# Gate stores issued by GpSimd, low-rank pieces fetched a tile ahead, features loaded in pieces, 49-point operands padded

## The chip, the cores and the metric

One core of a Trainium2 chip. The metric is device microseconds of one launch; less is better.

## What is computed

Three blocks, each feeding the next, on tensors of batch 2, 3136 tokens, 256 features (float32):

```python
# 1 attention with squared ReLU scores, gated by u
attn = np.maximum(np.matmul(z, z.transpose(0, 2, 1)) / S, 0.0) ** 2
x = u * np.matmul(attn, v)
# 2 low-rank token mixing (rank 32), then a channel MLP of width 1024
u1 = x + (x.transpose(0, 2, 1) @ U @ V).transpose(0, 2, 1)
y = u1 + np.maximum(u1 @ w_ch1, 0.0) @ w_ch2
# 3 2-D Fourier mixing (tokens and features), layer norm, a second channel MLP
u2 = y + np.real(np.fft.fft(np.fft.fft(y, axis=1), axis=2))
un = (u2 - mean(u2)) / np.sqrt(var(u2) + 1e-6)
out = u2 + np.maximum(un @ w2_ch1, 0.0) @ w2_ch2
```

U, V and the MLP weights arrive as float64 and are converted on the chip. Every large product is made of three matmuls: operands are split into an upper part `h` and a remainder `l` (ScalarE copies to the upper part, VectorE subtracts), and h·h, h·l and l·h are summed in PSUM. The 3136-point token transform is a 64 x 49 split; `b49h` and `b49l` are the two parts of the 49-point matrix, 98 rows (49 points, two parities) by 128 columns.

## The kernel before

Tokens are cut into seven chunks of 448 (`CH`) per batch. The program has two parts, each with an order of work written out by hand as Python generators that are advanced step by step. Within a part every engine keeps the written order; where the two parts meet, a queue can take the second part's instruction first if the first part's is not yet free to run.

*Attention.* For each of 14 (batch, chunk) pairs there are 13 steps (`order`), one per pair of key tiles; the seventh step is the odd tile 12, half as wide. In a step `ahead` issues the score matmuls for two steps later (`LAG`), ScalarE takes ReLU (L542) and square (L545), VectorE casts to `h` (L546) and subtracts for `l` (L96, the line of the helper `sub`), and `values` does the 24 matmuls onto the accumulators (L568). On the eleventh key tile of each pair, `gate` multiplies with u and writes the result to DRAM twice: feature-major to `aT_d` by one DMA (L599) and, after a 32 x 32 transpose by VectorE (L602), token-major to `aN_d` by eight DMAs (L606). Each of those eight moves 32 partitions x 14 blocks x 32 floats. All of them are issued by SP (`load` is `nc.sync.dma_start`, `late_dma` is `nc.gpsimd.dma_start`), and SP also issues all the loads of the following steps: queries, keys, values and u, and `stg`, the weight blocks that the `conversions` jobs turn from float64 into float32. A DMA instruction on SP holds up what is written behind it.

During the second batch's attention, `lowrank` makes the 64 x 256 sum U^T x of the first batch: 13 pieces of up to 256 tokens, each loaded from `aN_d` (L620), split, and multiplied (L632) into a score bank. A piece takes four of the generator's turns: load and two yields, split and one yield, matmuls and one yield. Generators get no turn in the last two steps of a pair.

*Channel mixers.* 28 chunks (two layers, two batches, seven chunks) of eight steps. A step i does `hidden(k)`, six matmuls of the first MLP matrix (L324 to L326), and `project(k)` of step i - 2, six of the second (L349 to L351). `Chunk.prep` of the next chunk runs beside it: for layer 1 it starts at step 2 of the chunk before, adds the low-rank term by two matmuls with the V rows (L244; the rows come by `Chunk.load`, two DMAs of GpSimd, L230) to the features `xT`. The features are loaded by `load_x` (L801) in four DMAs, of 1344, 1344, 1568 and 1568 tokens, all issued before the first step. Beside the first steps `mixer` makes the low-rank sum of the second batch: 13 pieces loaded from `aN_d` into the two buffers of `wst` (L812), split into `nh` and `nl`, and multiplied (L825) one tile per step, the first in its fourth turn. `fourier(b)` later transposes 98-column pieces by TensorE (L868), splits them into 98 partitions of `nh`, `nl` and multiplies by `b49h`, `b49l` (L875 to L877). `starts` says at which step a generator begins; TensorE's program is in order, so a matmul of a generator that waits holds up those of the MLP behind it.

Of the kernel before, what the change touches and what calls it, by code (L numbers as in the profile page):

```python
# [21 lines left out]
CH = 448  # L22
# [60 lines left out]
def program(ctx, tc, zT, v, uT, U, V, w1a, w2a, w1b, w2b, b49, f64, fd, rep, mask, out):  # L83
# [8 lines left out]
    def hcopy(o, i):  # L92
        nc.scalar.copy(o, i)  # L93
# [33 lines left out]
    b49h = const.tile([98, 128], F32R, name="b49h")  # L127
    b49l = const.tile([98, 128], F32R, name="b49l")
# [8 lines left out]
    def constants(t):  # L137
        make_identity(nc, ident)
        load(out=repc, in_=rep)
        load(out=maskc, in_=mask)  # L140
        load(out=t[0:98, 0:128], in_=b49)
        load(out=f64s, in_=f64)
        load(out=t[:, 256:768], in_=fd)
        nc.vector.memset(t[:, 768:896], 1.0 / D)
        for _ in range(5):
            yield
        hcopy(ones, t[:, 768:896])
        hcopy(b49h, t[0:98, 0:128])
        sub(b49l, t[0:98, 0:128], f(b49h))
        for dst, k in ((fA, 256), (fB, 384)):  # L150
            hcopy(dst[:, 0], t[:, k : k + 128])
            sub(dst[:, 1], t[:, k : k + 128], f(dst[:, 0]))
        hcopy(fN, t[:, 512:768].rearrange("p (a n) -> p a n", a=2))
# [226 lines left out]
    def attention(stack):  # L380
# [209 lines left out]
        def gate(b, qc):  # L590
            last = (b, qc) == (1, NC - 1)
            t, tb = (ptile() if last else att.tile([128, 2 * CH], F32, tag="aT", name="aT") for _ in range(2))
            o, u = acc.pop((b, qc)), uq.pop((b, qc))
            for a in range(2):
                hcopy(c2(t)[:, a], o[a][0][:, 0:CH])
                tt(out=c2(t)[:, a], in0=o[a][1][:, 0:CH], in1=c2(t)[:, a], op=ALU.add)
            tt(out=c2(t), in0=c2(t), in1=u, op=ALU.mult)
            tokens = slice(qc * CH, qc * CH + CH)
            load(out=aT_d[b][:, :, tokens].rearrange("a p n -> p a n"), in_=c2(t))  # L599
            yield  # L600

            nc.vector.transpose(out=tb, in_=t)  # L602
            for a in range(2):
                for i in range(4):
                    o = a * 128 + i * 32
                    load(  # L606
                        out=aN_d[b][tokens, o : o + 32].rearrange("(j t) d -> t j d", t=32),
                        in_=c2(tb)[i * 32 : i * 32 + 32, a].rearrange("p (j d) -> p j d", d=32),
                    )
            yield  # L610

        def lowrank():
# [3 lines left out]
            for k in range(0, 25, 2):  # L616
# [4 lines left out]
                yield  # L621
                yield
# [5 lines left out]
                yield  # L628
# [12 lines left out]
                yield  # L641
# [129 lines left out]
    def pair_late():  # L771
        return [late["mp"].tile([128, 512], F32R, tag=t, name=t) for t in ("nh", "nl")]

# [24 lines left out]
    late["small"] = small  # L798

# [3 lines left out]
    def mixer():  # L803
# [3 lines left out]
        for k in range(28):  # L807
# [18 lines left out]
            yield  # L826
        P = small()[:, 0:D]
# [8 lines left out]
    def fourier(b):  # L836
# [27 lines left out]
        def tokens(i):  # L864
# [4 lines left out]
            h, l = (t[0:98] for t in pair_late())  # L869
            hcopy(h, ps[0:98, :])  # L870
            sub(l, ps[0:98, :], f(h))
# [14 lines left out]
        def column128():  # L886
# [3 lines left out]
            h, l = (t[0:98, 0:32] for t in pair_late())  # L890
            hcopy(h, ps[0:98, 0:32])
            sub(l, ps[0:98, 0:32], f(h))
# [158 lines left out]
    with tc.manual_schedule():  # L1051
        nstep = len(chunks) * 8
        active = []
        starts = {
            20: weights(0), 50: fourier(0), 106: fourier(1), 13 * 8: weights(1),
# [3 lines left out]
        for b, s, e in ((0, CH, 1792), (0, 1792, S), (1, 0, 1568), (1, 1568, S)):  # L1059
            load_x(b, s, e)  # L1060
        mix1 = mixer()
        active.append(mix1)
        for i in range(nstep + 2):
# [17 lines left out]
            if i in starts:  # L1081
                active.append(starts[i])
            for g in list(active):
# [49 lines left out]
```

## Time and profile before

| | us |
|---|---|
| median of 3 runs (lowest, highest) | 1226.63 (1224.61, 1229.32) |
| the profiled execution's own time | 1227.88 |
| its span, first to last instruction | 1226.1 |
| TensorE busy | 1175.5 |
| VectorE busy | 853.0 |
| ScalarE busy | 658.8 |
| GpSimd busy | 53.0 |
| mean granted TensorE clock | 0.986 |

Engines: PE is TensorE's matmuls, PEld its weight loads, DVE VectorE, ACT ScalarE, POOL GpSimd, SP SyncE. An engine name with a q is its sequencer, which waits or issues. A granted clock of 1.00 is 2.4 GHz, 0.50 is 1.2 GHz. Matmuls overlap in the record: one of 448 columns is shown with 0.36 us, while the next starts 0.20 us after it, or 0.10 us where two of 64 rows run side by side. So a busy TensorE need not be at its full pace.

### The profile page before, as it was taken

How to read it: one execution, taken by the hardware profiler on the slowest of the kernel's cores; microseconds unless marked ns; L12 is line 12 of the kernel's file. 1: busy time of each engine (PE TensorE's matmuls, PEld its weight loads, DVE VectorE, ACT ScalarE, POOL GpSimd, SP SyncE). 2: the span in 40 equal slices, each digit the busy share in tenths (PEclk: the TensorE clock that was granted, in tenths of full speed). 3: DMA queues.
4: the chain of work that ended last, by engine and by line, in shares of the span. 5: the costliest groups of instructions: out<-in, count | busy, mean ns of one | idle time of the engine just before them, and what ended most of it. 6: DMA issues, size and time to landing. Idle time of an engine off the chain costs nothing.

```text
span 1226.1 us, 21429 instructions
## 1 busy us (share of the span) xinstructions
PE 1175.5 (96%) x8454; PEld 1069.4 (87%) x8454; DVE 853.0 (70%) x1611; ACT 658.8 (54%) x1089; POOL 53.0 (4%) x104
## 2 busy tenths in 40 slices
PE   9999999899999998999499999999999999999998
PEld 8888898789889887999499899999998989899997
DVE  7877787667788887877355646466566688766674
ACT  7877777667676766766133324333255444444442
POOL 0000100000000000000000000020000111000000
PEclk9999999999999999999799999999999999999999
DMA  4313432133243233223722001111012211111111
GB/s 141 84 33 83 101 78 64 36 105 100 53 106 88 74 92 105 75 62 78 250 58 73 25 16 43 59 40 40 8 36 73 60 41 33 38 31 38 31 39 45
DMA packets 116659, 80.79 MB, mean 66 GB/s; under 512 B 63630, under 2 KB 110640, under 8 KB 116560
## 3 DMA queue, kind: packets, MB, share of 16 engines
q1 hardware_dynamic: 110448, 71.94, 20.4%
q0 software_dynamic: 5696, 7.31, 2.8%
q8 instruction: 66, 1.08, 0.4%
q14 instruction: 33, 0.27, 0.1%
q10 hardware_dynamic: 416, 0.20, 0.1%
HBM read 52.94 MB, written 26.39 MB: 65 GB/s over the span
## 4 chain that ended last, share of the span: by engine, by line
PE 68%; DVE 12%; ACT 7%; DMA 6%; SPq 4%; issue 3%; DVEq 0%; ACTq 0%
PE psO L568 20%; PE psH L324 7%; PE psH L326 6%; PE psH L325 6%; PE psC L349 6%; PE psC L350 6%; PE psC L351 6%; PE psS L536 5%; SPq L606 3%; ACT P L542 3%; ACT P L545 2%; DVE l L96 2%; DVE h L546 1%; DVE aT L602 1%; DVE Hl L330 1%
## 5 line engine op out<-in xcount | busy, mean ns | idle before, releaser
L568 PE MATMUL psO<-h,Vt 64*128 64x448 f32 x2744 | 438.0, 368 | 5.4 <-DVE h L546 5.0
L568 PEld LDWEIGHTS psO<-h,Vt 64*128 64x128 f32 x2744 | 289.8, 187 | 27.7 <-DVE h L546 8.4
L568 PE MATMUL psO<-l,Vt 64*128 64x448 f32 x1372 | 287.1, 371 | 6.5 <-DVE l L96 6.4
L330 DVE SCALAR_TENSOR_TENSOR Hl<-psH,Hh 128x448 fp32r<-128x448 f32 x224 | 138.8, 622 | 156.2 <-ACT Hh L329 155.2
L96 DVE TENSOR_TENSOR l<-P,h 128x896 fp32r<-128x896 f32 (+2 forms) x211 | 210.0, 995 | 23.7 <-ACT h L93 16.5
L329 ACT ACTIVATE Hh<-psH 128x448 fp32r<-128x448 f32 x224 | 121.2, 542 | 180.3 <-PE psH L326 177.8
L542 ACT ACTIVATE P<-psS 128x896 f32<-128x896 f32 (+1 forms) x183 | 161.0, 880 | 46.5 <-PE psS L536 44.6
L568 PEld LDWEIGHTS psO<-l,Vt 64*128 64x128 f32 x1372 | 153.8, 187 | 23.5 <-DVE l L96 15.2
L545 ACT ACTIVATE P<-P 128x896 f32<-128x896 f32 (+1 forms) x183 | 168.4, 921 | 5.7
L324 PE MATMUL psH<-h,w 128*128 128x448 f32 x448 | 168.1, 375 | 0.0
L326 PE MATMUL psH<-h,w 128*128 128x448 f32 x448 | 164.6, 367 | 0.0
L325 PE MATMUL psH<-l,w 128*128 128x448 f32 x448 | 164.5, 367 | 0.0
L349 PE MATMUL psC<-Hh,w 128*128 128x448 f32 x448 | 163.9, 366 | 0.3 <-DVE P L372 0.2
L350 PE MATMUL psC<-Hl,w 128*128 128x448 f32 x448 | 163.6, 365 | 0.4 <-DVE Hl L330 0.4
L351 PE MATMUL psC<-Hh,w 128*128 128x448 f32 x448 | 162.7, 363 | 0.0
L546 DVE CAST h<-P 128x896 fp32r<-128x896 f32 (+1 forms) x183 | 110.3, 603 | 70.3 <-ACT P L545 68.3
L536 PE MATMUL psS<-Q,KT 64*128 64x448 f32 x1002 | 135.3, 367 | 5.6 <-ACT P L542 3.1
L536 PEld LDWEIGHTS psS<-Q,KT 64*128 64x128 f32 x1002 | 100.5, 186 | 13.8 <-ACT P L542 4.2
L349 PEld LDWEIGHTS psC<-Hh,w 128*128 128x128 f32 x448 | 84.2, 188 | 8.3 <-issue 1.2
L350 PEld LDWEIGHTS psC<-Hl,w 128*128 128x128 f32 x448 | 84.3, 188 | 8.2 <-DVE Hl L330 1.4
L324 PEld LDWEIGHTS psH<-h,w 128*128 128x128 f32 x448 | 84.6, 189 | 7.4 <-issue 0.3
L326 PEld LDWEIGHTS psH<-h,w 128*128 128x128 f32 x448 | 84.4, 188 | 7.4
(290 smaller groups left out, 1147.3 us busy)
## 6 DMA issues: line engine op xcount, KB each, us to landing
uT<-in_uT SPq DMA_DIRECT2D x14, 448.0 KB, 4.4
vraw<-in_v SPq DMA_DIRECT2D x24, 256.0 KB, 2.9
out<-P SPq DMA_DIRECT2D x27, 224.0 KB, 2.0
aTd<-aT SPq DMA_DIRECT2D x13, 448.0 KB, 3.0
aNd<-aT SPq DMA_DIRECT2D x104, 56.0 KB, 1.9
scr<-wst SPq DMA_DIRECT2D x16, 256.0 KB, 2.0
Vs<-Vd POOLq DMA_DIRECT2D x28, 112.0 KB, 2.5
xT<-aTd SPq DMA_DIRECT2D x2, 1568.0 KB, 10.9
```

Source lines behind the costliest of these rows:

```text
L96: tt(out=o, in0=a, in1=b, op=ALU.subtract)
L324: mm(ps[:, 0:CH], wh, self.h[:, a], start=a == 0, stop=False)
L325: mm(ps[:, 0:CH], wh, self.l[:, a], start=False, stop=False)
L326: mm(ps[:, 0:CH], wl, self.h[:, a], start=False, stop=a == 1)
L330: stt(out=l, in0=ps[:, 0:CH], scalar=0.0, in1=f(h), op0=ALU.max, op1=ALU.subtract)
L349: mm(dst, wh, h, start=k == 0, stop=False)
L350: mm(dst, wh, l, start=False, stop=False)
L351: mm(dst, wl, h, start=False, stop=k == 7)
L536: mm(ps[:, j, 0:w], k, q[r, kq, o : o + w], start=(kk, kq) == (0, 0), stop=kk == 1)
L542: act(out=dst, in_=ps[:, j : j + m, 0:w], func=AF.Relu, scale=1.0 / S)
L545: act(out=A[:, x], in_=A[:, x], func=AF.Square)
L568: mm(o[fa][i][:, 0:CH], vt[r, j, k, fa * 128 : fa * 128 + 128], x[r, j * CH : j * CH + CH], start=p == 0 and n == 0, stop=p == 11 and n == ...
```

## The change

The DMAs of `gate` go from SP to GpSimd, and each is issued one turn later: the feature-major store after the first yield, the eight token-major ones after a new yield behind the transpose. In `lowrank` a piece is loaded when the one before it has been split, and there are two yields between split and matmuls; a piece still takes four turns. `load_x` before the first mixer step loads tokens 448 to 1344 of batch 0 alone; the rest comes in six pieces of up to 896 tokens at steps 4, 12, 26, 34, 42 and 50. `mixer` begins at step 4 instead of before step 0. `b49h`, `b49l` get 128 rows, with zeros below row 98; `nh` and `nl` become two fixed pairs of tiles, whose rows 96 to 127 GpSimd clears after the mixer's matmuls, and the 49-point matmuls take all 128 rows.

```diff
--- before.py
+++ after.py
@@ -124,8 +124,8 @@
     ident = const.tile([128, 128], F32, name="ident")
     repc = const.tile([128, 128], F32, name="repc")
     maskc = const.tile([128, 6], F32, name="maskc")
-    b49h = const.tile([98, 128], F32R, name="b49h")
-    b49l = const.tile([98, 128], F32R, name="b49l")
+    b49h = const.tile([128, 128], F32R, name="b49h")
+    b49l = const.tile([128, 128], F32R, name="b49l")
     f64s = const.tile([128, 128], F32, name="f64s")
     fA = const.tile([128, 2, 128], F32R, name="fA")
     fB = const.tile([128, 2, 128], F32R, name="fB")
@@ -145,8 +145,10 @@
         for _ in range(5):
             yield
         hcopy(ones, t[:, 768:896])
-        hcopy(b49h, t[0:98, 0:128])
-        sub(b49l, t[0:98, 0:128], f(b49h))
+        for x in (b49h, b49l):
+            nc.gpsimd.memset(f(x), 0.0)
+        hcopy(b49h[0:98], t[0:98, 0:128])
+        sub(b49l[0:98], t[0:98, 0:128], f(b49h[0:98]))
         for dst, k in ((fA, 256), (fB, 384)):
             hcopy(dst[:, 0], t[:, k : k + 128])
             sub(dst[:, 1], t[:, k : k + 128], f(dst[:, 0]))
@@ -596,14 +598,15 @@
                 tt(out=c2(t)[:, a], in0=o[a][1][:, 0:CH], in1=c2(t)[:, a], op=ALU.add)
             tt(out=c2(t), in0=c2(t), in1=u, op=ALU.mult)
             tokens = slice(qc * CH, qc * CH + CH)
-            load(out=aT_d[b][:, :, tokens].rearrange("a p n -> p a n"), in_=c2(t))
-            yield
+            yield
+            late_dma(out=aT_d[b][:, :, tokens].rearrange("a p n -> p a n"), in_=c2(t))

             nc.vector.transpose(out=tb, in_=t)
+            yield
             for a in range(2):
                 for i in range(4):
                     o = a * 128 + i * 32
-                    load(
+                    late_dma(
                         out=aN_d[b][tokens, o : o + 32].rearrange("(j t) d -> t j d", t=32),
                         in_=c2(tb)[i * 32 : i * 32 + 32, a].rearrange("p (j d) -> p j d", d=32),
                     )
@@ -613,19 +616,28 @@

             g = att.tile([64, D], F32, tag="G", name="G", bufs=1)
             nc.vector.memset(g, 0.0)
-            for k in range(0, 25, 2):
+
+            def fetch(k):
                 w = 2 if k < 24 else 1
                 t0 = 128 * k if k < 24 else S - 128
                 raw = att.tile([128, 2, D], F32, tag="an", name="an", bufs=1)[:, 0:w]
                 load(out=raw, in_=aN_d[0][t0 : t0 + 128 * w].rearrange("(s p) d -> p s d", p=128))
-                yield
-                yield
+                return raw
+
+            raw = fetch(0)
+            for k in range(0, 25, 2):
+                w = 2 if k < 24 else 1
+                for _ in range(2):
+                    yield
                 h, l = (
                     att.tile([128, 2, D], F32R, tag=t, name=t, bufs=1)[:, 0:w] for t in ("anh", "anl")
                 )
                 hcopy(h, raw)
                 sub(l, raw, f(h))
-                yield
+                if k < 24:
+                    raw = fetch(k + 2)
+                for _ in range(2):
+                    yield
                 ps = psS.tile([128, 2, 512], F32, tag="S", name="psS")
                 for n in range(2 * w):
                     for i, r in enumerate(halves):
@@ -638,7 +650,7 @@
                         )
                 for i in range(2):
                     tt(out=g, in0=ps[0:64, i, 0:D], in1=g, op=ALU.add)
-                yield
+            yield
             yield
             ps = psS.tile([128, 2, 512], F32, tag="S", name="psS")
             mm(ps[:, 0, 0:D], repc[0:64], g, start=True, stop=True)
@@ -768,9 +780,6 @@
         active.clear()
         assert not active and next(jobs, None) is None

-    def pair_late():
-        return [late["mp"].tile([128, 512], F32R, tag=t, name=t) for t in ("nh", "nl")]
-
     with ExitStack() as st, tc.manual_schedule():
         attention(st)

@@ -796,6 +805,12 @@
         return mp.tile([128, CH], dt, tag="sm", name="sm", bufs=4)

     late["small"] = small
+
+    nats = [[mp.tile([128, 512], F32R, tag=f"{t}{k}", name=f"{t}{k}", bufs=1) for t in ("nh", "nl")] for k in range(2)]
+
+    def pair_late():
+        nats.append(nats.pop(0))
+        return nats[-1]

     def load_x(b, s, e):
         load(out=xT[b][:, :, s:e], in_=aT_d[b][:, :, s:e].rearrange("a p n -> p a n"))
@@ -824,6 +839,9 @@
                 for j, x in enumerate(parts.pop(0)):
                     mm(g, uu, x, start=k == 3 and j == 0, stop=k == 27 and j == 1)
             yield
+
+        for x in (*nats[0], *nats[1]):
+            nc.gpsimd.memset(f(x)[96:128], 0.0)
         P = small()[:, 0:D]
         nc.vector.memset(P[64:128], 0.0)
         nc.vector.tensor_copy(P[0:64], g)
@@ -866,9 +884,9 @@
             ps = misc()
             for s in range(4):
                 nc.tensor.transpose(ps[0:98, s * 128 : s * 128 + 128], y[:, s * 98 : s * 98 + 98], ident)
-            h, l = (t[0:98] for t in pair_late())
-            hcopy(h, ps[0:98, :])
-            sub(l, ps[0:98, :], f(h))
+            h, l = pair_late()
+            hcopy(h[0:98], ps[0:98, :])
+            sub(l[0:98], ps[0:98, :], f(h[0:98]))
             nat[i] = (h, l)

         def dft49(ps, h, l):
@@ -887,9 +905,9 @@

             ps = misc()
             nc.tensor.transpose(ps[0:98, 0:128], raw128, ident)
-            h, l = (t[0:98, 0:32] for t in pair_late())
-            hcopy(h, ps[0:98, 0:32])
-            sub(l, ps[0:98, 0:32], f(h))
+            h, l = (t[:, 0:32] for t in pair_late())
+            hcopy(h[0:98], ps[0:98, 0:32])
+            sub(l[0:98], ps[0:98, 0:32], f(h[0:98]))
             yield
             ps = misc()
             dft49(ps[:, 0:32], h, l)
@@ -1051,15 +1069,14 @@
     with tc.manual_schedule():
         nstep = len(chunks) * 8
         active = []
+        mix1 = mixer()
         starts = {
-            20: weights(0), 50: fourier(0), 106: fourier(1), 13 * 8: weights(1),
+            4: mix1, 20: weights(0), 50: fourier(0), 106: fourier(1), 13 * 8: weights(1),
         }
         calm = [starts[50], starts[106]]

-        for b, s, e in ((0, CH, 1792), (0, 1792, S), (1, 0, 1568), (1, 1568, S)):
-            load_x(b, s, e)
-        mix1 = mixer()
-        active.append(mix1)
+        load_x(0, CH, 3 * CH)
+        fetches = {4: (0, 3), 12: (0, 5), 26: (1, 0), 34: (1, 2), 42: (1, 4), 50: (1, 6)}
         for i in range(nstep + 2):
             c, k = divmod(i, 8)
             if i < nstep:
@@ -1080,6 +1097,9 @@
                 chunks[c + 2].load()
             if i in starts:
                 active.append(starts[i])
+            if i in fetches:
+                b, k = fetches[i]
+                load_x(b, k * CH, min(k * CH + 2 * CH, S))
             for g in list(active):
                 if k == 0 and g in calm:
                     continue
```

## Rows read from the trace of the kernel before

**Rows 1.** The page's slices: tenths of TensorE busy in 40 equal parts of the span.
```profile
PE   9999999899999998999499999999999999999998
```

**Rows 2.** Windows: from:to, length, each engine's busy us (instructions), granted clock, DMA share, GB/s.
```profile
587.90:595.60 7.70, 7.69 (x37) 6.60 (x36) 4.57 (x7) 2.06 (x4) 1.15 (x4) 1.00 0.87 267
595.60:611.40 15.80, 0.19 (x1) 0.00 (x0) 0.00 (x1) 0.44 (x2) 0.00 (x0) 0.58 0.93 339
611.40:615.10 3.70, 3.68 (x10) 3.10 (x11) 1.38 (x3) 1.17 (x3) 0.00 (x0) 0.51 0.21 68
560.00:580.00 20.00, 20.00 (x202) 19.89 (x200) 13.62 (x22) 13.05 (x16) 0.00 (x0) 1.00 0.25 56
55.34:557.28 501.94, 477.34 (x4581) 433.05 (x4579) 394.01 (x659) 352.19 (x487) 6.08 (x10) 0.98 0.30 80
270.32:277.14 6.82, 6.35 (x34) 5.22 (x36) 5.50 (x8) 3.88 (x7) 0.00 (x0) 0.50 0.30 97
```

**Rows 3.** TensorE's timeline at the seam: start us, us, what, idle before and releaser.
```profile
611.42 0.48 PE L825 MATMUL ps_g<-nh,Uhl 128*64 128x256 f32 x1 [15.63 <-ACT nh L93]
```

**Rows 4.** ScalarE's timeline at the seam.
```profile
610.96 0.40 ACT L93 CAST nh<-wst 128x256 fp32r<-128x256 f32 x1 [18.55 <-DMA wst<-aNd]
```

**Rows 5.** SP's timeline at the seam.
```profile
588.05 0.37 SPq L801 DMA_DIRECT2D xT<-aTd  x1
...
591.52 5.02 SPq L606 DMA_DIRECT2D aNd<-P  x8
596.59 1.52 SPq L801 DMA_DIRECT2D xT<-aTd  x3
598.21 37.66 SPq L812 DMA_DIRECT2D wst<-aNd  x7
```

**Rows 6.** SP's timeline behind the sixth gate.
```profile
259.14 4.83 SPq L606 DMA_DIRECT2D aNd<-aT  x8
264.01 0.48 SPq L445 DMA_DIRECT2D vraw<-in_v  x1
```

**Rows 7.** ScalarE's timeline behind the same gate.
```profile
267.06 0.62 ACT L93 CAST Vt<-vraw 128x512 fp32r<-128x512 f32 x1 [5.17 <-DMA vraw<-in_v]
...
268.53 0.95 ACT L545 ACTIVATE P<-P 128x896 f32<-128x896 f32 x1
```

**Rows 8.** VectorE's timeline behind the seventh gate.
```profile
312.55 0.29 DVE L163 TENSOR_SCALAR stg<-stg 128x256 uint16<-128x256 uint16 x1 [4.51 <-DMA stg<-in_w2a]
...
313.61 1.09 DVE L96 TENSOR_TENSOR l<-P,h 128x896 fp32r<-128x896 f32 x1
```

**Rows 9.** TensorE's groups, 0 to 590: line, names, count | busy us, mean ns | idle before.
```profile
L632 PE MATMUL psS<-anl,Uhl 64*64 64x256 f32 x50 | 7.1, 295 | 6.7 <-DVE anl L96 6.7
```

**Rows 10.** GpSimd's timeline at the seam.
```profile
583.34 1.03 POOL L230 DMA_DIRECT2D Vs<-Vd  x2 [434.32 <-PE psS L655]
590.54 0.18 POOL L793 MEMSET raw<- 128x98 f32 x1 [6.17 <-DVE P L597]
```

**Rows 11.** GpSimd's groups over the span, its DMA issues.
```profile
L230 POOL DMA_DIRECT2D Vs<-Vd x28 | 14.6, 528 | 672.5 <-PE psS L655 434.3 <-PE ps_x L244 107.8 <-PE ps_m L244 70.1
L316 POOL DMA_DIRECT2D rs<-rsd x14 | 8.3, 596 | 22.5 <-DMA rsd<-vy 22.5
...
L488 POOL DMA_DIRECT2D Vd<-stg x8 | 5.0, 624 | 141.5 <-ACT stg L93 134.8 <-DVE stg L163 4.5 <-DVE stg L96 2.1
```

**Rows 12.** VectorE's timeline: a cast beside GpSimd's DMAs, and one without.
```profile
148.18 0.73 DVE L546 CAST h<-P 128x896 fp32r<-128x896 f32 x1 [1.21 <-ACT P L545]
...
575.92 0.63 DVE L546 CAST h<-P 128x896 fp32r<-128x896 f32 x1 [0.68 <-ACT P L545]
```

**Rows 13.** GpSimd's timeline beside that cast.
```profile
147.93 1.09 POOL L230 DMA_DIRECT2D Vs<-Vd  x2
```

**Rows 14.** TensorE's groups, 640 to the end: first and second matmul of a 49-point triple.
```profile
L875 PE MATMUL ps_g<-nh,b49h 98*128 98x512 f32 x6 | 2.9, 481 | 0.0
...
L876 PE MATMUL ps_g<-nl,b49h 98*128 98x512 f32 x6 | 2.4, 395 | 0.0
```

## The prediction, as put on record before the result was known

> **What bounds the kernel now.** I read the page's slices first: TensorE is busy nine tenths or more in 36 of 40, and the only low one, a 4, is the twentieth, 582 to 613 us [rows 1]. So TensorE is the bound, and a change is worth what it takes out of TensorE's stops and its stretches at half clock. A busy row hides part of that, since its matmuls overlap in the record, so I counted matmuls per stretch. An undisturbed 20 us of the attention holds 202; from the first gate's transpose at 55.34 to the thirteenth at 557.28 there are 4581 in 501.94 us [rows 2]. At 202 per 20 us these take 453.6: 48.3 us are lost in the attention, over twelve gate periods of 42 us.
>
> The low slice is the seam between attention and channel mixer. From 595.6 TensorE does next to nothing for 15.8 us and runs the next 3.7 us at 1.2 GHz, half of its 2.4 [rows 2]. The first matmul of the second low-rank sum (L825) waited 15.63 us for ScalarE's split, which sat 18.55 us waiting for its DMA [rows 3, 4]. SP's timeline says why: one feature load, the last gate's eight token-major stores, three more feature loads, and only at 598.21 the sum's first piece [rows 5]. Behind the seam every slice but the last is a 9 again [rows 1]: what is won there is not given back at once.
>
> For the attention I asked which late DMAs ended idle stretches of ScalarE and VectorE. SP sits in L606 from 259.14 for 4.83 us, the load behind it leaves at 264.01 [rows 6], and ScalarE, in order, idles 5.17 us for it [rows 7]; at a later gate VectorE idles 4.51 us for a weight block [rows 8]. TensorE stops soon after, as the scores go through these two engines. The low-rank matmuls stop it too: 6.7 us of idle before the fifty that wait for VectorE's lower half [rows 9].
>
> **The change part by part.** The profiled execution took 1227.88 us for a span of 1226.1; the median of the runs is 1226.63, 1.25 below. The sum is made against 1227.9.
>
> *A, the seam.* Before, three loads of 1344, 1568 and 1568 KB (1 KB per token) stand ahead of the first 256 KB piece: 4.85 MB at that stretch's 339 GB/s [rows 2] is 14.3 us from 596.6, which is the 610.9 at which ScalarE got it [rows 4]. After, SP has no gate store; it loads two pieces of 896 KB, then the sum's. Its first issue waited for TensorE's last attention matmul, at 588 [rows 5], and still does. 2.1 MB plus the gate's own 0.92 MB from the other queue is 3.0 MB, 8.9 us at 339 GB/s: landed by 597. The sum now starts at step 4, splits first at step 6 and multiplies first at step 7. Steps 0 to 3 end at 595.6, as now; a step is 12 matmuls at 7.70/37 us [rows 2], 2.5 us, so the split is due near 600.9, the matmul near 605.7. With 3 us of margin I take the whole hole, 15.8. Its half-clock tail goes too: 10 matmuls in 3.70 us [rows 2] where 7.70/37 each make 2.1, so 1.6. A = -17.4; bounds 0 (something else fills the hole) and -17.4.
>
> Chunk 1 also needs its V rows from POOL, where nine gate stores now stand too. POOL issued them at 583.34, ahead of buffer clears (590.54) that are written before them but were not yet free to run [rows 10]; SP's first feature load likewise went ahead of the gate's stores [rows 5]. A queue takes what is ready first, so I expect the V rows to pass the stores. If not, rival 2.
>
> *B, stalls behind late loads.* A gate takes SP 4.83 us of issue after a wait for the transpose; all 104 small stores leave SP for POOL. The loads behind them leave 5 to 8 us earlier, and idle stretches like those of [rows 7, 8] have no cause. The low-rank piece is fetched a round (4 steps) ahead instead of 2 steps, and its split stands two steps ahead of its matmuls instead of one: 3 us more (30 matmuls at 202 per 20 us). Of the 48.3 us 8 are C; 40 remain. Not all goes: step 12 of each period has half-width scores and six value matmuls, so a step behind it needs its probabilities after 4 us, and the chain that makes them takes 4.2 (six score matmuls 0.6, ScalarE 0.95 twice [rows 7], VectorE 0.63 and 1.09 [rows 8, 12]); conversions keep getting in between. I take half: B = -20. Bounds: -7, if only the waits of [rows 9] go, and -36.
>
> *C, half clock in the attention.* The mean clock there is 0.98, by its rounding 7.5 to 12.5 us of full speed gone; the longest stretch, at 270 behind the 5.17 us wait, did 34 matmuls in 6.82 us, half the pace of 202 in 20 [rows 2]. I count 8 lost, in four such stretches. Without the long stops before them three of the four go: C = -6; bounds 0 and -8.
>
> *D, the stores on POOL.* A token-major store has 448 pieces of 128 B; no POOL DMA here has so many. POOL is busy 0.528 us for one with 64 pieces (Vs), 0.596 with 128 (rs), 0.624 with 128 (Vd) [rows 11]. The lower end is 0.53, the upper, in proportion, 448/128 x 0.624 = 2.2. I take the slope of the first two, 0.07 per 64 pieces: 0.6 + 5 x 0.07 = 0.95, as these rows show mostly a fixed part. A gate then holds POOL 8 x 0.95 + 0.7 = 8.3 us of 42; it was busy 6 of 502 [rows 2]. Behind them in that queue stand only the V stores of four conversions and, at the end, the V rows of chunk 2, due 20 us later. A cast beside two POOL DMAs took 0.73 us against 0.63 without [rows 12, 13]. 8.3 us meets 3 casts per gate, 13 gates, 0.1 each: 4 us of VectorE, half of it on TensorE's path: D = +2; bounds 0 and rival 4's price.
>
> The Trainium skill (SBUF — State Buffer, "Who interferes with whom") says that a VectorE instruction in a two-port mode and GpSimd lock each other out for a whole instruction, whoever is first. This cast disagrees with a lock of that length: it lost 0.1 us beside two issues of 0.55. By the rule a cast would wait out a store: that is rival 4.
>
> *E, the rest, at 0.* Padding to 128 rows leaves 512 columns per matmul and 128 per weight load. The first matmul of a triple takes 481 ns, the second 395 [rows 14]; the first follows four short transposes that can't hide its weight load, and that stays. At most 16 x 0.09 = 1.4 us. The clears cost an idle POOL 3 us. The six later feature pieces carry the bytes they did and leave 16 steps (40 us) or more before use. The sum ends four steps later, near step 35; its result is needed at step 50.
>
> Sum: -17.4 - 20 - 6 + 2 = -41.4, so 1186.5 for an execution like the profiled one, 1185.2 for the median: 1186.
>
> **The rivals.**
> 1. *Only the seam.* The gate periods are bound by the chain of ScalarE and VectorE, and late loads merely show up in it. For: VectorE is busy 394 of 502 us [rows 2]. Against: its idle time ends on DMAs. B is -7, C 0, D +2: 1205; with B at 0, 1212. The Trainium skill (DMA: Bandwidth & Descriptors, "Issuing engines are not separate DMA queues") sides with it: issuing from another engine saves only issue time, usually small. The rows show a queue in order, where 4.83 us of issue became 5.17 of idle [rows 6, 7].
> 2. *The hole is filled again.* If chunk 1's V rows come behind the nine stores, they leave at 591.5 + 8.3 and land 3 us later (as the load of [rows 6, 7]), 602.8, for a matmul due at 597.8: 5 us; at 2.2 us a store 15 us and the half clock, the whole of A. 1191 to 1204.
> 3. *All goes*, B at -36 and C at -8: 1168.
> 4. *Slower: the casts wait for POOL.* At 2.2 us per store a gate holds POOL 19 us, meeting 6 casts (one per 2.97 us). If each waits half a store, 1.1 us, that is 6.6 us per gate, 86 in all; VectorE's idle time takes half, B and C don't come: 1227.9 - 17.4 + 43 = 1254. It decides from 3.2 us per gate (41.4/13). Against it: the 0.1 us of [rows 12].
>
> **How the numbers follow.** Forecast 0.60 (its own range 1174 to 1199), rival 1 0.14, rival 2 0.10, rival 3 0.06, rival 4 0.06, nothing gained 0.04. The range 1172 to 1212 holds the forecast, rivals 1 and 2; it leaves out 0.16 and a little of the forecast. Within 0.5% (6 us, about what a measurement of this kernel can tell from no change) is 1220 to 1233. Faster 0.89, same 0.05, slower 0.06.
>
> **What would show it.** A: the first L825 has no idle time, no half clock at 598, the sum's first piece lands before 600. B: gate periods near 40 us; ScalarE's and VectorE's waits for vraw, zraw, stg and an nearly gone; L632's idle time under 2 us. C: a granted clock of 1.00 through the attention. D: token-major stores near 0.95 us on POOL, casts near 0.65. Wrong: periods unchanged though the loads leave early (rival 1), a wait for Vs at step 4 (rival 2), casts over 1 us beside POOL's stores (rival 4).

## The result: 1225.6 us before, 1179.5 us after

The changed kernel takes 1179.51 us (median of 4 runs, 1179.1 to 1180.99), the kernel before beside it 1225.62 (1224.2 to 1229.32); the ratio is 0.9622 [0.9597, 0.9646]. In a second comparison of five rounds it took 1179.11 us (1178.48 to 1180.76), ratio 0.9595 [0.9572, 0.9619]. The profiled execution took 1179.2 us for a span of 1177.4.

**The page after.** Busy time of each engine, then the slices that answer to [rows 1], and the clock in the same 40 slices.

```profile
PE 1161.7 (99%) x8454; PEld 1061.9 (90%) x8454; DVE 854.6 (73%) x1611; ACT 659.2 (56%) x1089; POOL 142.2 (12%) x236
...
PE   9999999999999999999999999999999999999998
...
PEclk9999999999999999999999999999999999999999
```

The 4 at the seam is a 9. The engines do the same work in 48.7 us less; only GpSimd has more, 142 for 53 us.

**Where the time came from.** Windows of the kernel after, columns as in [rows 2]: first gate's transpose to the thirteenth's, to the fourteenth's, and the seam.

```profile
54.70:527.90 473.20, 466.73 (x4582) 427.82 (x4580) 394.96 (x659) 352.27 (x487) 79.89 (x116) 1.00 0.30 83
...
54.70:560.50 505.80, 499.33 (x4891) 459.96 (x4888) 419.68 (x694) 371.17 (x511) 87.26 (x128) 1.00 0.30 82
...
558.20:600.00 41.80, 41.80 (x214) 38.11 (x214) 22.08 (x40) 14.87 (x33) 9.10 (x17) 1.00 0.45 139
```

Twelve gate periods with 4582 matmuls take 473.20 us where 4581 took 501.94, at a clock of 1.00 where it was 0.98. The fourteenth gate's transpose stands at 560.5 instead of 590.4 (both from VectorE's timeline): 29.9 us of the 48.7 came before it, 18.8 behind it. In the seam TensorE has no idle time.

**The seam after.** SP's timeline, to be held against [rows 5]:

```profile
558.31 0.88 SPq L816 DMA_DIRECT2D xT<-aTd  x2
560.55 0.89 SPq L827 DMA_DIRECT2D wst<-aNd  x2
```

GpSimd's, against [rows 10]: the V rows of chunk 1 leave ahead of the gate's stores, those of chunk 2 behind them.

```profile
553.71 1.05 POOL L232 DMA_DIRECT2D Vs<-Vd  x2 [18.07 <-PE psS L667]
560.77 0.74 POOL L602 DMA_DIRECT2D aTd<-P  x1 [6.01 <-DVE P L599]
561.92 4.52 POOL L609 DMA_DIRECT2D aNd<-P  x7 [0.41 <-DVE P L604]
...
571.56 1.09 POOL L232 DMA_DIRECT2D Vs<-Vd  x2 [1.14 <-PE ps_x L246]
```

ScalarE's first split and TensorE's first low-rank matmul, against [rows 4] and [rows 3]; neither has a wait in front (no bracket).

```profile
573.03 0.40 ACT L93 CAST nh<-wst 128x256 fp32r<-128x256 f32 x1
```

```profile
576.03 0.28 PE L840 MATMUL ps_g<-nh,Uhl 128*64 128x256 f32 x1
```

**The attention after.** SP's own waits in the attention (line, what for: us in all, times, longest), first before, then after.

```profile
SPq L599 <- DVE aT L597: 183.7, 13, 28.9
SPq L606 <- DVE aT L602: 53.2, 13, 5.1
```

```profile
POOL aTd L602 <- DVE aT L599: 359.4, 13, 49.7
POOL aNd L609 <- DVE aT L604: 57.3, 11, 6.1
```

The waits for VectorE's gate work have moved from SP to GpSimd. Groups of VectorE, ScalarE, TensorE and GpSimd in the attention, the last column being the idle time in front: VectorE's and ScalarE's waits for late loads, first before, then after.

```profile
L163 DVE TENSOR_SCALAR stg<-stg 128x256 uint16<-128x256 uint16 (+3 forms) x41 | 11.4, 279 | 18.2 <-DMA stg<-in_w2a 4.9 <-DMA stg<-in_U 3.9 <-DMA stg<-in_w2b 3.1
...
L93 ACT CAST Vt<-vraw 128x512 fp32r<-128x512 f32 (+1 forms) x13 | 7.8, 597 | 10.3 <-DMA vraw<-in_v 10.2
```

```profile
L165 DVE TENSOR_SCALAR stg<-stg 128x256 uint16<-128x256 uint16 (+3 forms) x41 | 11.7, 285 | 2.0 <-DMA stg<-in_w1b 0.9 <-DMA stg<-in_w2b 0.7 <-DMA stg<-in_w1a 0.3
...
L93 ACT CAST Vt<-vraw 128x512 fp32r<-128x512 f32 (+1 forms) x13 | 7.7, 592 | 1.6 <-DMA vraw<-in_v 1.6
...
L538 PE MATMUL psS<-Q,KT 64*128 64x448 f32 x912 | 124.7, 365 | 4.3 <-DVE G L652 4.3
...
L644 PE MATMUL psS<-anl,Uhl 64*64 64x256 f32 x50 | 6.4, 275 | 0.0
...
L609 POOL DMA_DIRECT2D aNd<-aT x104 | 70.8, 689 | 63.7 <-DVE aT L604 57.3 <-DVE h L548 6.1 <-issue 0.4
```

Idle time of VectorE and ScalarE that a DMA ended, summed over such rows, falls from 44.4 to 5.9 us; TensorE's idle time in the windows above falls from 24.6 to 6.5.

### The profile page after: what moved, and what is told of

It reads as the page before. It is cut to its first block, busy times and chain, and to the rows that moved or that the text cites. A ratio compares the mean times of both kernels' runs of the same rounds, so it can differ in the third digit from the quotient of the medians.

```text
span 1177.4 us, 21521 instructions
## 1 busy us (share of the span) xinstructions
PE 1161.7 (99%) x8454; PEld 1061.9 (90%) x8454; DVE 854.6 (73%) x1611; ACT 659.2 (56%) x1089; POOL 142.2 (12%) x236
## 4 chain that ended last, share of the span: by engine, by line
PE 71%; DVE 12%; ACT 8%; issue 6%; DMA 2%; SPq 0%; POOL 0%; DVEq 0%; POOLq 0%; ACTq 0%
PE psO L570 21%; PE psH L326 7%; PE psH L328 7%; PE psH L327 7%; PE psC L351 7%; PE psC L352 7%; PE psC L353 7%; PE psS L538 5%; ACT P L547 3%; DVE l L96 3%; ACT P L544 3%; DVE h L548 2%; ACT stg L168 1%; DVE Hl L332 1%; ACT stg L169 1%
## 5 line engine op out<-in xcount | busy, mean ns | idle before, releaser
L570 PE MATMUL psO<-h,Vt 64*128 64x448 f32 x2744 | 432.9, 363 | 0.5
L570 PEld LDWEIGHTS psO<-h,Vt 64*128 64x128 f32 x2744 | 285.1, 184 | 18.9 <-DVE Vt L96 1.9
L570 PE MATMUL psO<-l,Vt 64*128 64x448 f32 x1372 | 282.5, 367 | 2.7 <-DVE l L96 2.4
L570 PEld LDWEIGHTS psO<-l,Vt 64*128 64x128 f32 x1372 | 151.2, 184 | 18.8 <-DVE l L96 10.7
```

Source lines behind the costliest of these rows:

```text
L570: mm(o[fa][i][:, 0:CH], vt[r, j, k, fa * 128 : fa * 128 + 128], x[r, j * CH : j * CH + CH], start=p == 0 and n == 0, stop=p == 11 and n == ...
```

## The experiments

My theory: two separate things were removed, the hole at the seam (by the pieces and the later start) and SP standing still in front of and in the gate's stores, behind which the loads came late. The low-rank fetch, the padding and GpSimd's own time count for little. The rivals are those of the prediction, and for each part of the change, that another part does its work. Four experiments take the change apart, the rest change one thing in the kernel after.

**1. Only the gate's stores moved** (in the kernel before):

```diff
-            load(out=aT_d[b][:, :, tokens].rearrange("a p n -> p a n"), in_=c2(t))
             yield
+            late_dma(out=aT_d[b][:, :, tokens].rearrange("a p n -> p a n"), in_=c2(t))
             nc.vector.transpose(out=tb, in_=t)
+            yield
...
-                    load(
+                    late_dma(
```

> The kernel before with the gate's stores alone moved to GpSimd and a turn later. If SP's queue is what makes loads late (the theory): gate periods fall from about 42 to about 40 us as in the changed kernel, at least three of the four half-clock stretches go, 22 to 28 us of gain in the attention. At the seam four feature loads (5.8 MB) still stand ahead of the sum's first piece, now without the eight stores: 6.1 MB and up to 0.9 MB of stores at 339 GB/s end 18 to 21 us after the loads may start, for a matmul due after 7.5, so the hole shrinks from 15.8 to 10.5 to 13. Time 1193 to 1201. If the chain of ScalarE and VectorE bounds the periods instead (the prediction's rival 1): no more than 7 us there, time 1215 to 1222.

Measured: 1196.96 us (1195.2 to 1198.01) beside 1228.75, ratio 0.9751 [0.972, 0.9782], so -31.8. The fourteenth transpose stands at 559.4, and no stretch of the attention has less than full clock. The hole is left, TensorE's timeline:

```profile
578.60 0.48 PE L826 MATMUL ps_g<-nh,Uhl 128*64 128x256 f32 x1 [13.82 <-ACT nh L93]
```

and its half clock, in a window around it:

```profile
568.00:581.70 13.70, 3.10 (x9) 2.57 (x10) 1.38 (x3) 1.14 (x3) 1.79 (x5) 0.50 0.76 293
```

So this edit makes the whole gain of the attention by itself and next to none at the seam: the hole is 13.8 us where it was 15.6, a little longer than the 10.5 to 13 expected. That speaks against rival 1.

Another reading would be that the loads land faster, since GpSimd's stores go out in fewer packets (last section). They do not: the page's row for the loads of values is the same in both kernels (the last number is the median from issue to landing, in us), the four kinds of weight blocks take 2.8 to 2.9 us in both, the other repeated loads differ by less than 1 us, some one way and some the other, and the DMA engines are busy 0.30 of the gate periods in both ([rows 2] and the window above). The loads leave earlier.

```profile
vraw<-in_v SPq DMA_DIRECT2D x24, 256.0 KB, 2.9
```

**2. Only the low-rank pieces fetched ahead** (in the kernel before, as in the change; its core):

```diff
                 hcopy(h, raw)
                 sub(l, raw, f(h))
-                yield
+                if k < 24:
+                    raw = fetch(k + 2)
+                for _ in range(2):
+                    yield
```

> The kernel before with the low-rank pieces alone fetched a tile ahead. Theory: the idle time before the L632 matmuls (8.4 us) goes to under 1, some of it comes back as waits for a score bank; the stretches behind late loads stay, but the one half-clock stretch that followed a late low-rank piece (441 us) goes. Time 1217 to 1222. If the low-rank stops were only another face of the same lateness, nothing measurable: 1223 to 1228.

Measured: 1229.64 us (1225.24 to 1233.21), ratio 1.0017 [0.9997, 1.0037]: nothing, and not the 1217 to 1222 of the theory. The waits of [rows 9] did go: no row of the low-rank matmuls has idle time left. They came back elsewhere, TensorE's groups in the attention and VectorE's wait for weight blocks:

```profile
L568 PE MATMUL psO<-l,Vt 64*128 64x448 f32 x1190 | 256.2, 374 | 7.0 <-DVE l L96 6.9
...
L536 PE MATMUL psS<-Q,KT 64*128 64x448 f32 x872 | 121.7, 372 | 10.6 <-DVE G L648 5.6 <-ACT P L542 4.9
...
L163 DVE TENSOR_SCALAR stg<-stg 128x256 uint16<-128x256 uint16 (+3 forms) x40 | 11.2, 279 | 22.7 <-DMA stg<-in_w2a 6.3 <-DMA stg<-in_w2b 5.3 <-DMA stg<-in_w1b 4.0
```

In the kernel before the score matmuls (L536) had 5.2 us there and the `l` matmuls 6.0. TensorE now waits for a free score bank, which VectorE's additions into G and ScalarE release. SP is as late as it was, only with other loads: ScalarE no longer idles for the low-rank piece (5.9 us in the kernel before), but VectorE idles 22.7 us for weight blocks, where it idled 18.2 (19.3 in experiment 3). The half clock at 441 us is gone, as expected; but it is gone in experiment 3 too, whose attention is the kernel before's, so it does not tell of the edit.

**3. Only the seam** (in the kernel before; the table `fetches` and its use as in the change):

```diff
-            20: weights(0), 50: fourier(0), 106: fourier(1), 13 * 8: weights(1),
+            4: mix1, 20: weights(0), 50: fourier(0), 106: fourier(1), 13 * 8: weights(1),
...
-        for b, s, e in ((0, CH, 1792), (0, 1792, S), (1, 0, 1568), (1, 1568, S)):
-            load_x(b, s, e)
-        mix1 = mixer()
-        active.append(mix1)
+        load_x(0, CH, 3 * CH)
```

> The kernel before with the feature loads in pieces and the mixer begun at step 4, the gate's stores left on SP. Theory: the hole of 15.8 us and its half-clock tail go although SP still issues the eight stores there: about 17 us, 1207 to 1211, attention unchanged. If the stores on SP are what fills the hole, 5 us of their issue remain in the way of the sum's first piece and the first matmul waits 3 us or more: 1212 to 1220.

Measured: 1210.62 us (1208.78 to 1211.38), ratio 0.9857 [0.983, 0.9884], -18.1. SP still issues the eight stores, and its timeline shows that they stand ahead of the sum's pieces without harm:

```profile
593.39 4.23 SPq L606 DMA_DIRECT2D aNd<-P  x8
597.66 0.49 SPq L801 DMA_DIRECT2D xT<-aTd  x1
598.26 0.94 SPq L812 DMA_DIRECT2D wst<-aNd  x2
```

ScalarE splits the first piece without a wait:

```profile
604.77 0.40 ACT L93 CAST nh<-wst 128x256 fp32r<-128x256 f32 x1
```

The three parts add up: 1228.75 - 31.8 + 0.9 - 18.1 = 1179.75, and the whole measured 1179.5. That one stood beside a lower median of the kernel before, 1225.62; in ratios, the product of the three is 0.963, the whole 0.962 and 0.960.

**4. The engine or the later turn?** The kernel after, its stores at the new turns but issued by SP:

```diff
-            late_dma(out=aT_d[b][:, :, tokens].rearrange("a p n -> p a n"), in_=c2(t))
+            load(out=aT_d[b][:, :, tokens].rearrange("a p n -> p a n"), in_=c2(t))
...
-                    late_dma(
+                    load(
```

> The changed kernel with the gate's stores at their new turns, but issued by SP. If the engine is what matters (theory): the loads written behind the stores are late again, about half to all of the gain of the attention is lost: 1188 to 1205. If the later turn alone does it: 1179 to 1184.

Measured: 1206.18 us (1203.26 to 1207.68), ratio 0.982 [0.9791, 0.9849], 26.7 above the kernel after and just over the range. VectorE's wait for weight blocks is back:

```profile
L165 DVE TENSOR_SCALAR stg<-stg 128x256 uint16<-128x256 uint16 (+3 forms) x41 | 11.5, 280 | 24.2 <-DMA stg<-in_w2a 7.6 <-DMA stg<-in_w2b 6.7 <-DMA stg<-in_w1b 3.1
```

It is the engine that makes the gain, not the turn: from the first to the fourteenth transpose this run takes 533.7 us, the kernel before 535.0, the kernel after 505.8. Its median lies 4.4 us under that of experiment 3, from which it differs by the turn, the low-rank edit and the padding; the turn has brought no more than about that. GpSimd with the old turn was not run.

**5. The kernel after again, and without the low-rank edit.** The first is the kernel after, unchanged; the second has `lowrank` as it was before:

```diff
                 load(out=raw, in_=aN_d[0][t0 : t0 + 128 * w].rearrange("(s p) d -> p s d", p=128))
-                return raw
...
+                yield
+                yield
```

> The changed kernel as it is, measured beside the next ones: 1179 to 1181 again.

> The changed kernel with the low-rank sum fetched as before. Alone on the old kernel that edit was worth nothing. Theory now: with SP free the pieces come in time in either order, the stops at L632 (4.3 us in the run with only the gate moved) are traded for waits on the score bank (4.3 us in the changed kernel): within 2 us of the changed kernel, 1178 to 1182. The prediction's step B, by which the edit brings some 7 us: 1185 to 1188.

Measured: 1179.11 us, as told above, and 1179.32 (1179.2 to 1182.42), ratio 0.9601 [0.9576, 0.9625]. With SP free, too, the edit is worth nothing. TensorE's groups in the attention without it:

```profile
L538 PE MATMUL psS<-Q,KT 64*128 64x448 f32 x918 | 123.7, 364 | 1.6 <-DVE G L644 1.6
L636 PE MATMUL psS<-anl,Uhl 64*64 64x256 f32 x50 | 6.9, 293 | 4.2 <-DVE anl L96 4.1
```

4.2 us in front of the low-rank matmuls and 1.6 for G, against 0.0 and 4.3 with the edit: one wait traded for another.

**6. Only one of the nine stores back on SP.** The kernel after, its feature-major store issued by SP at its old place:

```diff
+            load(out=aT_d[b][:, :, tokens].rearrange("a p n -> p a n"), in_=c2(t))
             yield
-            late_dma(out=aT_d[b][:, :, tokens].rearrange("a p n -> p a n"), in_=c2(t))
```

> The changed kernel with the feature-major store of the gate back on SP at its old turn, the eight token-major ones on GpSimd. Theory: what made SP late is the wait for the transpose and the 4.8 us of eight issues; the one store costs 0.4 us and a shorter wait, so most of the gain stays: 1179 to 1185. If any store in SP's order that waits for the gate is enough to make the loads late: 1190 to 1206, as with all nine on SP.

Measured: 1180.99 us (1180.6 to 1181.67), ratio 0.961 [0.9584, 0.9636], 1.5 to 1.9 above the kernel after. SP's waits in the attention:

```profile
SPq L601 <- DVE aT L599: 173.5, 13, 28.2
```

and ScalarE's wait for values:

```profile
L93 ACT CAST Vt<-vraw 128x512 fp32r<-128x512 f32 (+1 forms) x13 | 7.7, 595 | 5.4 <-DMA vraw<-in_v 5.4
```

SP stands 173.5 us at that store and it costs under 2 us. What cost some 25 (experiment 4 against this run) was the shorter stop behind it: in the kernel before 53.2 us for the transposes and then eight issues, 4.83 us in [rows 6], with a load of values behind them for which ScalarE then idled [rows 7]. That it matters when SP stops, and not how long, is argued from these two runs; the wait and the issues of the eight stores were not tried apart.

**7. The pieces or the later start?** Both are the kernel after with one half of the seam's edit undone: e5 begins the mixer at turn 0, e6 loads the features in four large transfers.

```diff
-            4: mix1, 20: weights(0), 50: fourier(0), 106: fourier(1), 13 * 8: weights(1),
+            20: weights(0), 50: fourier(0), 106: fourier(1), 13 * 8: weights(1),
...
         load_x(0, CH, 3 * CH)
+        active.append(mix1)
```

> The kernel after, but the channel mixer begun at turn 0 of the last chunk's step as before, with its features in the six pieces. Theory (the hole is the time until the first piece's 0.9 MB have landed): the sum's first piece lands about 5 us after its issue near 558, so the later start is hardly needed: a hole of 0 to 2 us, 1179 to 1182 us. Rival (the later start is what closes it, and whatever is loaded early lands with the weights, 18 us after the issue): a hole of 8 us or more, 1187 to 1196 us.

```diff
-        load_x(0, CH, 3 * CH)
-        fetches = {4: (0, 3), 12: (0, 5), 26: (1, 0), 34: (1, 2), 42: (1, 4), 50: (1, 6)}
+        for b, s, e in ((0, CH, 1792), (0, 1792, S), (1, 0, 1568), (1, 1568, S)):
+            load_x(b, s, e)
+        fetches = {}
```

> The kernel after, but the features loaded by four large transfers as before, with the mixer begun at turn 4. Theory (the first split needs all of 6.1 MB, at the 339 GB/s of [rows 2] 18 us, with the stores beside it up to 20.7): they land at 576 to 579 for a matmul due near 571 to 576: a hole of 3 to 9 us and some half clock, 1183 to 1189 us. Rival (the later start alone closes the seam, since the issue no longer stands behind the rows of V): no hole, 1179 to 1181 us. Second rival (large transfers are what fills the hole, wherever they are begun): 1193 us or more.

Measured: 1181.17 us (1180.45 to 1181.36), ratio 0.9601 [0.9584, 0.9617], and 1186.93 (1185.99 to 1187.83), ratio 0.9651 [0.9631, 0.9671]. In e5 ScalarE has the first piece 5.6 us after the seam's first load was issued at 557.96, 3.2 after its own:

```profile
563.56 0.41 ACT L93 CAST nh<-wst 128x256 fp32r<-128x256 f32 x1 [1.24 <-DMA wst<-aNd]
```

and TensorE has no stop there. In e6 it has one, with 6.8 us of half clock in it and behind it (from 577.8):

```profile
580.79 0.47 PE L840 MATMUL ps_g<-nh,Uhl 128*64 128x256 f32 x1 [4.93 <-ACT nh L93]
```

The pieces close the hole. The later start adds 1.7 to 2.1 us to them, and without them it leaves 7.4 to 7.8 (both against the two medians of the kernel after). The size of e6 came out as expected, but its cause has a part I had not seen: of the 22 us until the piece was there, SP stood 9.1 at the fourth feature load, which reads what the last gate's feature-major store had yet to write.

```profile
SPq L816 <- DMA aTd<-P: 9.1, 1, 9.1
```

**8. Each token-major store twice** (the second by GpSimd too, into a tensor that nothing reads; it doubles D):

```diff
+                    late_dma(
+                        out=aD_d[b][tokens, o : o + 32].rearrange("(j t) d -> t j d", t=32),
+                        in_=c2(tb)[i * 32 : i * 32 + 32, a].rearrange("p (j d) -> p j d", d=32),
+                    )
```

> The kernel after with each of the 104 token-major stores issued a second time by GpSimd, into a tensor that nobody reads. Theory (GpSimd has some 1000 us idle and nobody waits behind a store): 70 us more of GpSimd's busy time and no change beyond 2 us, 1179 to 1182 us. Rival (GpSimd's stores hold up VectorE's casts, or the bytes the loads): VectorE's casts longer than their 0.63 us and at least 10 us more, 1190 to 1200 us.

Measured: 1184.68 us (1183.7 to 1185.45), ratio 0.963 [0.9613, 0.9647], 5.2 to 5.6 above the kernel after: between the two expectations, and neither cause. The casts are no longer in the mean: VectorE's groups in the attention, by form, after and here.

```profile
L548 DVE CAST h<-P 128x896 fp32r<-128x896 f32 x155 | 97.6, 630 | 60.7 <-ACT P L547 59.8
```

```profile
L549 DVE CAST h<-P 128x896 fp32r<-128x896 f32 x155 | 97.7, 631 | 59.9 <-ACT P L548 58.9
```

One gate period of thirteen is longer, the third, 42.7 us against 38.4. GpSimd's, SP's, VectorE's and TensorE's timelines in it:

```profile
146.30 1.36 POOL L491 DMA_DIRECT2D Vd<-stg  x2
```

```profile
149.26 0.89 SPq L498 DMA_DIRECT2D stg<-in_w1a  x2
```

```profile
152.16 0.29 DVE L166 TENSOR_SCALAR stg<-stg 128x256 uint16<-128x256 uint16 x1 [3.17 <-DMA stg<-in_w1a]
```

```profile
153.25 0.48 PE L571 MATMUL psO<-h,Vt 64*128 64x448 f32 x2 [1.73 <-DVE h L549]
```

Two V stores of a conversion stand behind sixteen gate stores. In the kernel after they leave one by one, the second at 142.99; here at 146.30. Their `stg` buffers come free that much later, SP's load into one leaves at 149.26 instead of 146.51, VectorE idles for it, TensorE stops and runs 3.4 us at half clock. So GpSimd's queue has the same fault as SP's had; it has it at one gate only, and only when held twice as long.

**9. One score bank for the low-rank pieces.** The remaining wait for G (4.3 us) comes from two banks and two additions per piece. e8 multiplies over all 128 rows into one bank and adds once; e11 gives the Fourier stretch a fifth small buffer as well (the room comes from one buffer of `wraw`, and `both` is taken from the small ones).

```diff
-                    for i, r in enumerate(halves):
-                        mm(
-                            ps[0:64, i, 0:D],
-                            Uhl[r, k + n // 2].rearrange("p h n -> p (h n)"),
-                            (h, l)[n % 2][r, n // 2],
+                    mm(
+                        ps[0:64, 0, 0:D],
+                        Uhl[:, k + n // 2].rearrange("p h n -> p (h n)"),
+                        (h, l)[n % 2][:, n // 2],
...
-                for i in range(2):
-                    tt(out=g, in0=ps[0:64, i, 0:D], in1=g, op=ALU.add)
+                tt(out=g, in0=ps[0:64, 0, 0:D], in1=g, op=ALU.add)
```

> The changed kernel with each low-rank piece multiplied over all 128 rows into one score bank, so that one addition per piece frees it instead of two. Theory (what is left of the low-rank stops is the score bank held until VectorE has added twice): the 4.3 us of waits on G fall to some 1 to 2, 1175 to 1179. If the wait is for VectorE's queue and not for the second addition: 1179 to 1181.

```diff
-        return mp.tile([128, CH], dt, tag="sm", name="sm", bufs=4)
+        return mp.tile([128, CH], dt, tag="sm", name="sm", bufs=5)
```

> The kernel of e8_one_bank with five instead of four of the small stage buffers that the Fourier stretch's loads use. Theory (the 2.4 us that the attention saves are given back because the Fourier stretch's load of vv starts only when a buffer comes free, and VectorE waits 2.8 us for it): the load starts earlier, 1176 to 1179 us. Rival (they are given back because VectorE is about 90% busy there and sets the pace): 1179 to 1181 us, like e8_one_bank.

Measured: e8 1180.84 us (1179.51 to 1182.17), ratio 0.9608 [0.9584, 0.9632]. The wait is gone (TensorE's groups), and the fourteenth transpose comes at 558.4, 2.4 earlier than in the kernel after run beside it:

```profile
L538 PE MATMUL psS<-Q,KT 64*128 64x448 f32 x920 | 121.1, 366 | 0.6 <-DVE G L650 0.6
```

The span is the same, 1177.7 for 1177.6, and the median 1.7 us above, with ranges that overlap. At least part of the 2.4 us is given back in the Fourier stretch, where VectorE waits 2.8 us for a small load (in the kernel after 1.3) and TensorE then for VectorE (in the kernel after 0.4):

```profile
L352 PE MATMUL psC<-Hl,w 128*128 128x448 f32 x66 | 24.3, 369 | 2.1 <-DVE Hl L332 2.1
```

With the fifth buffer VectorE's wait for that load is gone, and e11 took 1177.78 us (1177.56 to 1179.44), ratio 0.9577 [0.956, 0.9594]. That is the lowest median of all, 1.3 us under the kernel after in a comparison of as many rounds, but the intervals overlap, and the profiled execution was the slowest of the four; its span (1177.5) does not show the gain. So it is not shown that the buffer gives the 2.4 us back. Nor is it sure that e8 had them: e11 has the same attention, and from the first to the fourteenth transpose it took 505.4 us there, 503.4 in e8, 505.8 and 506.0 in two executions of the kernel after.

## Why the prediction was right

It said 1186 with the likeliest case at -41.4; measured were -46.1 in the medians and -48.7 in the profiled spans, within its range. Of the 7.3 us that the profiled spans gained beyond the sum, 5.2 lie in the attention, 1.4 at the seam and 0.6 ahead of the first gate. By its steps:

- *A, the seam, -17.4.* -18.8 behind the fourteenth transpose, -18.1 alone, both a little beyond the bound. The expected marks are there: no idle time before the first L840, no half clock, the V rows ahead of the stores. The matmul was put at 605.7; with all that comes before it 29.9 us earlier that is 575.8, and it came at 576.03. The step took the later start as a condition ("with 3 us of margin"); e5 shows that the pieces alone close the hole, at 1.7 to 2.1 us more.
- *B and C, -26 together.* From the first gate's transpose to the fourteenth's 535.0 us became 505.8, -29.2 with D in it. The clock's part is the whole of the 8 us counted, not 6: all four stretches went, with the stops that stood in front of them. That leaves some -21 for B, where -20 was put. That is in part luck: the -20 was half of 40, taken and not worked out. The reason given for the half that stays, the chain behind the short step, hardly shows: in the kernel after TensorE has no idle time for `h` and 2.1 us for `l`.
- *B's inner working was wrong in one place.* It gave the waits of [rows 9] to the low-rank edit ("if only the waits of [rows 9] go", -7). The waits went and the time stayed, alone (ratio 1.0017) and inside the change (experiment 5). In the kernel before a late load was part of them, ScalarE's group:

```profile
L93 ACT CAST anh<-an 128x512 fp32r<-128x512 f32 (+1 forms) x13 | 7.7, 593 | 5.9 <-DMA an<-aNd 5.9
```

With the edit alone that wait went, and SP was late with the weight blocks instead (experiment 2). With SP free nobody waits for the piece in either order, and 4.2 us before the low-rank matmuls or 4.3 before the score matmuls remain; what makes VectorE late there was not shown. The bound was read off an idle column without asking what else would be late.

- *D, +2.* Too little to measure. A token-major store holds GpSimd 0.69 us, not 0.95, and the casts take 630 ns where they took 623 (VectorE's group before, by form): 155 x 0.007 = 1.1 us of an engine with 61 us of idle time in front of these casts.

```profile
L546 DVE CAST h<-P 128x896 fp32r<-128x896 f32 x155 | 96.6, 623 | 63.4 <-ACT P L545 61.5 <-PE psS L536 0.9
```

The prediction looked at the casts alone, but it is mostly the stores that wait. GpSimd's timeline in e10, a store during which a cast begins, and VectorE's:

```profile
143.40 1.03 POOL L610 DMA_DIRECT2D aNd<-aT  x1
```

```profile
143.57 0.63 DVE L549 CAST h<-P 128x896 fp32r<-128x896 f32 x1 [1.22 <-ACT P L548]
```

In the kernel after, the 49 stores beside a cast take 0.74 us in the mean and up to 1.41, the other 63 take 0.64; of the 155 casts the 53 beside a GpSimd instruction take 0.64 us and up to 0.83, the others 0.62. The Trainium skill (SBUF — State Buffer, "Who interferes with whom") has a VectorE instruction in a two-port mode and GpSimd lock each other out for whole instructions. The longest stores look like it; whether these casts run in such a mode no run here shows. Rival 4 falls, since no cast waits out a store of 0.64 us; the price that doubling has (5 us) comes from the queue.

- *E, 0.* The first matmul of a padded triple takes 484 ns (481 before), the second 396 (395).
- *Rival 1* leaned on the rule of the Trainium skill (DMA: Bandwidth & Descriptors, "Issuing engines are not separate DMA queues") that another issuing engine saves only issue time, usually small. The trace agrees with the first half: loads did not get faster (values land 2.9 us after issue in both kernels), they left earlier. It was not small: SP was rid of some 4.83 us of issue per gate and of the waits in front of it, and moving the stores saved 31.8 us.

What stays open: the kernel after still needs 505.8 us for 4891 matmuls which at 202 per 20 us [rows 2] are 484.3. Of these 21.5 us only 6.5 are idle time of TensorE; where the rest goes was not tried.

## What to carry to other kernels

When a store waits for work that is done late, look at what stands behind it in its queue rather than at what it costs: give it to an engine whose queue holds nothing urgent, and check the few things that remain behind it there, as experiment 8 shows. At a seam between two parts, count the bytes issued ahead of the first piece that TensorE needs, and split the large loads until that piece has little in front. An idle column does not say what an edit will bring: where another wait ends just behind it, nothing. Try the edit alone before keeping it.

## What the runs showed of the hardware

The same store goes out in other packets from GpSimd. The page's DMA row before, after, and with the stores doubled, and in the last two the row of GpSimd's queue:

```profile
DMA packets 116659, 80.79 MB, mean 66 GB/s; under 512 B 63630, under 2 KB 110640, under 8 KB 116560
```

```profile
DMA packets 66853, 80.81 MB, mean 69 GB/s; under 512 B 13502, under 2 KB 57408, under 8 KB 66752
...
q0 software_dynamic: 10848, 20.16, 7.6%
```

```profile
DMA packets 70437, 87.24 MB, mean 74 GB/s; under 512 B 15294, under 2 KB 59200, under 8 KB 70336
...
q0 software_dynamic: 14432, 26.59, 10.9%
```

The bytes stay and 50128 packets under 512 B go, about the 112 x 448 = 50176 pieces of the token-major stores: SP sent one packet per 128 B piece. The second copy of the 112 stores adds 3584 packets, 32 each: 16 under 512 B and 16 between 2 and 8 KB, none between. The 56 KB of a store in 16 packets are 3584 B each, the pieces of two of its 32 partitions. They land later than SP's all the same (median 2.6 us after issue, 1.9 before), and GpSimd's time per issue hardly follows the pieces: 0.69 us for 448, where [rows 11] have 0.53 for 64.
